# Blank matmuls between the first transposes, a step moved ahead of a transpose, and one slot more for the arrival of loads, in a kernel of two sliding-window attention blocks

## The chip, the cores and the metric

The kernel runs on one core of a Trainium2 chip. The metric is the device time in microseconds (us) of one execution. The engines are TensorE (PE; its weight loads are shown as PEld), VectorE (DVE), ScalarE (ACT), GpSimd (POOL) and SyncE (SP), which here issues nearly all of the transfers.

## The reference

Two independent problems A and B of the same form are computed, and their outputs are put side by side. Each is a multi-head attention block with a causal sliding window:

```
B, S, D = 1, 2048, 1024;  H = 32 heads;  Dh = 32;  W = 256
q, k, v = split(x @ wqkv)                      # each S x D, in heads of 32
scores = (q @ k.T) * Dh**-0.5                  # per head
mask   = (0 <= i - j) & (i - j < W)            # query i, key j
p      = softmax(where(mask, scores, -1e9))
out    = concat_heads(p @ v) @ wo              # S x D
result = concat([out_A, out_B], axis=-1)
```

All inputs and outputs are bf16.

## The kernel before, in words

Sequence positions are cut into 16 blocks of 128, and these into four groups of four (512 positions, index k). Heads are taken four at a time (a head group g, 128 columns of q, k or v; eight for each problem, 16 in all). x is held transposed, as `xT[(problem, k)]` with 8 slices of 128 input columns (`ct`), because TensorE contracts over partitions.

Projections are cut into chains (`_Chain`): a chain for Q or K of one head group and 512 positions is eight matmuls, one for each `ct`, accumulated in one PSUM bank (`qk_steps`, tile `pp`, two buffers), then copied out by ACT or DVE (`evacuate`, line 188). V chains (`v_steps`) serve two head groups (index m) and two blocks, in 16 matmuls of 256 columns. Chains of the output projection (`out_steps`, `last_steps`) end in a store. `by_columns` (line 170) issues a step either as one matmul (line 172) or as four of 32 columns that run side by side (line 176).

Attention runs in 180 slots, the loop over `now` from line 600. In each slot, `session` (line 438) computes scores of four block pairs for four heads (line 451, PSUM tile `st`, one buffer), ACT takes their exponentials (line 459, tile `pt`), and POOL clears what the mask forbids (lines 467 and 471). Three slots later `pv` (line 486) multiplies with V and with ones, the second for the sums of the softmax (line 513, tile `acc`). DVE adds edge blocks (line 481), takes the reciprocal of the sums (line 524), spreads it (line 529) and multiplies (line 531).

What is left of a slot on TensorE is filled with steps of chains, by a planner that runs when the program is built. Each chain has an `early` and a `late` slot. `start_chain` takes the ready chain (`early <= now`) with the smallest `late`. `level` (line 426) sets how many nanoseconds of work a slot gets, from the listed durations `NS_MM`, `NS_ROW` and `NS_PV`. Its result is the smallest, over later slots d, of the work that becomes ready before d divided by the slots up to d; work with a later `early` is so kept out of the sum for smaller d.

Loads after the first are cut into pieces and put into slots by the loop at line 331. POOL writes a zero to the piece's place (line 350), which orders it, and SP issues the load: for B's x as transposing transfers (line 133), in two pieces for each block. The dictionary `arrival` holds the slot from which chains may use a load: the slot of its last piece plus 2. `landed` (line 342) hands it to the chains' `early` (lines 360, 365 and 375). The x of problem A and the first weights have arrival slots set by hand (lines 328 and 329).

The head of the program is written out by hand. ACT's queue issues the first Q weights. SP's queue issues, in this order, x blocks 0 and 1 as plain rows, the first K weights, x blocks 2 and 3, V weights, then transposing loads of A's later x groups with weights between them (lines 541 to 562). While these come in, TensorE runs five matmuls on a blank tile of zeros (`top`, seen as `blank`, lines 564 to 566). Then `flip(a)` transposes block a on TensorE (eight transposes of 128 by 128 into one PSUM bank, line 578), and ACT (line 582) and after it DVE (line 583) copy a half each into `xT[(0, 0)]`. `first(which, lo)` (line 585) does the eight steps of the first Q (0) or K (1) chain for 256 of its 512 columns: columns 0 to 255 need flips 0 and 1, columns 256 to 511 need flips 2 and 3. The last of these is followed by the first V chain.

Of the kernel before, what the change touches and what calls it, by code (L numbers as in the profile page):

```python
# [18 lines left out]
P = 128  # L19
# [59 lines left out]
def _fast_path(ctx, tc, cfg, problems, outs, consts, certify):  # L79
    nc = tc.nc  # L80
# [40 lines left out]
    xT, wqk, wv, wo_sb, vts, oTs, qks, pts = {}, {}, {}, {}, {}, {}, {}, {}  # L121
# [4 lines left out]
    blank = top[:].bitcast(BF16)  # L126
# [71 lines left out]
    def qk_steps(g, which, k, lo=0, hi=512, st_=None, last=True):  # L198
        pi = g // T
        st_ = {} if st_ is None else st_  # L200
        steps = []
        for ct in range(CT):
            def f(ct=ct):
                if "pp" not in st_:
                    st_["pp"] = new_pp()
                by_columns(st_["pp"], lo, hi, wqk[g][:, ct, which, :], xT[(pi, k)][:, ct, lo:hi],
                           ct == 0, ct == CT - 1)
                clock.pe += NS_MM * (hi - lo) / 512.0
                if ct == CT - 1 and last:
                    dst = qk_tiles(g)[which][:, k * 512:(k + 1) * 512]  # L210
                    evacuate(dst, st_["pp"][:])
                    add_or(dst)
            steps.append((NS_MM * (hi - lo) / 512.0, f))
        return steps
# [108 lines left out]
    def entries_of(now):  # L323
        return [(n // NE,) + entries[n % NE]
                for n in range(now * SLOTS, min((now + 1) * SLOTS, G * NE))]

    pieces = {}
    arrival = {("x", 0, k): t for k, t in ((2, 3), (3, 5))}
    arrival.update({("wqk", 1): 1, ("wv", 1): 4})
    free = 0  # L330
    for time, key, fs in wanted:
        free = max(free, time)
        new = fs[0]
        for where, f in fs[1:]:
            while len(pieces.get(free, [])) >= min(2 if key[0] == "x" else SLOTS, sum(
                    q != j + 1 for _, j, q in entries_of(free))):
                free += 1
            pieces.setdefault(free, []).append((new, where, f))
            new = None
        arrival[key] = free + 2  # L340

    def landed(*key):
        return arrival.get(key, 0)
# [218 lines left out]
            load_wv(1, 0, CT, nc.sync)  # L562

    warm = ps_proj.tile([P, 512], F32, name="pp")
    for _ in range(5):
        nc.tensor.matmul(warm[:], lhsT=blank[:, 0:P], rhs=blank[:, 0:512], start=True, stop=True)
    flips = [ps_acc.tile([P, 512], F32, name="acc") for _ in range(2)]
    flips = [f[:] for f in flips]
    flips.append(ps_st.tile([P, 4, SLOTS, P], F32, name="st")[:, 0].rearrange("p a q -> p (a q)"))
# [3 lines left out]
    def flip(a):  # L573
        if a == 3:
            flips[a] = ps_acc.tile([P, 512], F32, name="acc")[:]
        f = flips[a].bitcast(BF16).rearrange("p (ct q) -> p ct q", q=P)
        for ct in range(CT):
            nc.tensor.transpose(out=f[:, ct, :], in_=xrow[a][:, ct * P:(ct + 1) * P],  # L578
                                identity=ident[:])
        dst = xT[(0, 0)][:, :, a * P:(a + 1) * P]  # L580
        half = CT // 2
        nc.scalar.copy(out=dst[:, :half, :], in_=f[:, :half, :])
        nc.vector.tensor_copy(out=dst[:, half:, :], in_=f[:, half:, :])

    def first(which, lo):
        for _, f in qk_steps(0, which, 0, lo, lo + 256, held[which], last=lo > 0):
            f()

    flip(0)
    flip(1)  # L590
    flip(2)
    first(0, 0)
    flip(3)
    first(1, 0)
    first(0, 256)
# [4 lines left out]
    for now in range(END):  # L600
# [3 lines left out]
        while due and due[0][0] <= now:  # L604
            _, pg, pk = due.pop(0)
# [14 lines left out]
    while due:  # L620
        _, pg, pk = due.pop(0)
# [132 lines left out]
def kernel(  # L754
# [48 lines left out]
    with tc.manual_schedule():  # L803
        with ExitStack() as fctx:
            _fast_path(fctx, tc, cfg, problems, outs, consts, [reduce_bits, decide])
# [40 lines left out]
```

## Time and profile before

| what | value |
|---|---|
| median of 9 runs | 612.51 us (611.1 to 614.17) |
| profiled execution, its own time | 612.31 us |
| its span, first to last instruction | 610.6 us |
| TensorE busy | 599.7 us, 98% |
| VectorE, ScalarE, GpSimd busy | 463.6, 445.2, 328.1 us |
| instructions | 28789 |

The span is the stretch that the profile's views are told in: a time in them counts from its start. In a view in order of time, a line gives the start, the duration of the group, the engine, the line of the program, the operation, what is written and what is read, shapes, and how many instructions were merged (x8). Behind it in brackets stands the idle time of the engine ahead of it and what ended that. A duration of a group ends with the drain of its last matmul; the distance from one start to the next is the time for which TensorE is taken. A line of the waits gives the total in microseconds, how often, and the longest. "SPq" is the queue of SP that issues transfers. Granted clock is the share of TensorE's full clock that the profile shows.

### The profile page before, as it was taken

What the parts mean: (1) busy time and instruction counts of PE and PEld (TensorE: products, weight loads), DVE (VectorE), ACT (ScalarE), POOL (GpSimd) and SP (SyncE); (2) the same over time, 40 slices, a digit from 0 to 9 for tenths busy, and PEclk for the clock granted to TensorE, in tenths of its full rate; (3) what the DMA queues carried; (4) which work ended last, traced back from release to release, by engine and by line L of the source; (5) the groups of instructions that cost most, each with busy time, mean ns of one, the idle gap of its engine ahead of it and who ended that gap; (6) DMA issues with size and microseconds to landing.
All of it is one profiled execution on the core that took longest, in us unless ns stands there. A gap on an engine that the chain in (4) does not pass through costs nothing.

```text
span 610.6 us, 28789 instructions
## 1 busy us (share of the span) xinstructions
PE 599.7 (98%) x12824; PEld 345.4 (57%) x12824; DVE 463.6 (76%) x1193; ACT 445.2 (73%) x382; POOL 328.1 (54%) x630
## 2 busy tenths in 40 slices
PE   7999999999999999999999999999999999999996
PEld 5555466656654765654565756755445664545443
DVE  1577888887899889878888889698987978897200
ACT  3777878888887777877777777777776878776332
POOL 0565666666656666565555656555565556555000
PEclk9999999999999999999999999999999999999999
DMA  9923110111015510444111000112011030113221
GB/s 242 172 76 103 37 38 4 38 38 39 3 33 85 111 25 6 87 97 99 37 38 38 21 21 2 39 37 81 2 57 44 3 106 20 55 52 125 71 78 64
DMA packets 86802, 35.47 MB, mean 58 GB/s; under 512 B 65552, under 2 KB 86160, under 8 KB 86672
## 3 DMA queue, kind: packets, MB, share of 16 engines
q1 hardware_dynamic: 85632, 33.31, 22.6%
q8 instruction: 102, 1.67, 1.1%
q10 hardware_dynamic: 1040, 0.26, 0.2%
q14 instruction: 28, 0.23, 0.1%
HBM read 17.83 MB, written 8.39 MB: 43 GB/s over the span
## 4 chain that ended last, share of the span: by engine, by line
PE 95%; ACT 2%; DMA 1%; issue 0%; SPq 0%; POOL 0%; ACTq 0%
PE pp L176 43%; PE pp L172 29%; PE acc L513 13%; PE st L451 10%; ACT pt L459 2%; DMA oT<-in_A_x_dram 1%; DMA xT<-in_B_x_dram 0%; ACT vt L190 0%; PE st L578 0%; ACT kT L190 0%; PE acc L578 0%; SPq L548 0%; POOL pt L471 0%; ACT qT L190 0%; SPq L145 0%
## 5 line engine op out<-in xcount | busy, mean ns | idle before, releaser
L459 ACT ACTIVATE pt<-st 128x2048 bf16<-128x2048 f32 x180 | 338.0, 1878 | 86.5 <-PE st L451 70.4
L471 POOL TENSOR_SCALAR_AFFINE_SELECT pt<-pt 128x512 bf16<-128x512 bf16 x224 | 155.9, 696 | 145.7 <-ACT pt L459 145.7
L467 POOL TENSOR_SCALAR_AFFINE_SELECT pt<-pt 128x512 bf16<-128x512 bf16 x256 | 179.3, 702 | 87.0 <-ACT pt L459 87.0
L524 DVE RECIPROCAL rinv<-acc 128x128 f32<-128x128 f32 x128 | 121.8, 952 | 57.1 <-PE acc L513 56.6
L176 PE MATMUL pp<-xT,wqk 128*32 128x512 bf16 x2728 | 164.1, 379 | 1.0 <-DVE both L481 0.7
L481 DVE TENSOR_TENSOR both<-pt 128x512 bf16<-128x512 bf16 x224 | 138.1, 656 | 0.0
L176 PEld LDWEIGHTS <-wqk 128*32 128x32 bf16 x2728 | 69.8, 97 | 55.9 <-DVE both L481 0.9
L172 PE MATMUL pp<-xT,wqk 128*128 128x512 bf16 (+1 forms) x358 | 82.6, 374 | 0.8 <-ACT kT L190 0.4
L176 PE MATMUL pp<-wv,xT 128*32 128x256 bf16 x2436 | 75.6, 273 | 0.0
L451 PE MATMUL st<-qT,kT 32*128 32x384 bf16 (+2 forms) x1488 | 71.5, 269 | 0.0
L176 PEld LDWEIGHTS <-xT 128*32 128x32 bf16 x2436 | 63.8, 97 | 5.2
L529 DVE STREAM_SHUFFLE wide<-rinv 128x128 f32<-128x128 f32 x256 | 64.5, 297 | 0.0
L513 PE MATMUL acc<-pt,vt 128*32 128x128 bf16 (+1 forms) x2160 | 63.4, 239 | 0.0
L172 PE MATMUL pp<-wo_sb,oT 128*128 128x512 bf16 (+1 forms) x288 | 62.4, 374 | 0.0
L451 PEld LDWEIGHTS <-kT 32*128 32x128 bf16 x1488 | 22.2, 92 | 65.3 <-issue 63.8
L190 ACT CAST osb<-pp 128x512 bf16<-128x512 f32 (+1 forms) x54 | 31.1, 576 | 38.4 <-PE pp L172 26.9
L531 DVE TENSOR_TENSOR oT<-acc,wide 128x256 bf16<-128x256 f32 x128 | 54.3, 424 | 4.4
L176 PE MATMUL pp<-wo_sb,oT 128*32 128x512 bf16 x928 | 54.6, 379 | 0.0
L172 PEld LDWEIGHTS <-wqk 128*128 128x128 bf16 x358 | 33.4, 99 | 36.8 <-issue 6.9
L172 PE MATMUL pp<-wv,xT 128*128 128x256 bf16 x415 | 51.0, 273 | 0.4 <-ACT kT L190 0.2
L513 PEld LDWEIGHTS <-vt 128*32 128x32 bf16 x2160 | 35.9, 96 | 26.3 <-issue 24.0
L172 PEld LDWEIGHTS <-xT 128*128 128x128 bf16 x415 | 38.9, 98 | 11.6 <-issue 5.1
(46 smaller groups left out, 382.2 us busy)
## 6 DMA issues: line engine op xcount, KB each, us to landing
out_dram<-osb SPq DMA_DIRECT2D x63, 128.0 KB, 1.8
wqk<-in_B_wqkv_dram SPq DMA_DIRECT2D x32, 128.0 KB, 2.6
wqk<-in_A_wqkv_dram SPq DMA_DIRECT2D x24, 128.0 KB, 2.7
wo_sb<-in_A_wo_dram SPq DMA_DIRECT2D x16, 128.0 KB, 2.2
wv<-in_B_wqkv_dram SPq DMA_DIRECT2D x16, 128.0 KB, 2.6
wo_sb<-in_B_wo_dram SPq DMA_DIRECT2D x16, 128.0 KB, 2.5
oT<-in_A_x_dram SPq DMA_DIRECT2D x4, 256.0 KB, 4.8
wv<-in_A_wqkv_dram SPq DMA_DIRECT2D x2, 512.0 KB, 5.0
```

The costliest lines, as they stand in the source:

```text
L172: nc.tensor.matmul(out[:, lo:hi], lhsT=lhsT, rhs=rhs, start=start, stop=stop, skip_group_check=True)
L176: nc.tensor.matmul(out[c:c + 32, lo:hi], lhsT=lhsT[:, c:c + 32], rhs=rhs, start=start, stop=stop, tile_position=(0, c), skip_group_check=True)
L190: nc.scalar.copy(out=out, in_=in_)
L451: nc.tensor.matmul(st[:, r, a:b, :], lhsT=kT[32 * r:32 * r + 32, j * P:(j + 1) * P], rhs=qT[32 * r:32 * r + 32, q * P:(q + b - a) * P], st ...
L459: nc.scalar.activation(out=pt[:, :, :n, :].rearrange("p r a q -> p r (a q)"), in_=st[:, :, :n, :].rearrange("p r a q -> p r (a q)"), func= ...
L467: nc.gpsimd.affine_select(out=blk, in_=blk, pattern=[[0, 4], [1, P]], compare_op=ALU.is_ge, fill=0.0, base=0, channel_multiplier=-1)
L471: nc.gpsimd.affine_select(out=blk, in_=blk, pattern=[[0, 4], [-1, P]], compare_op=ALU.is_gt, fill=0.0, base=0, channel_multiplier=1)
L481: nc.vector.tensor_tensor(out=both[:, :, h, :], in0=pts[s0][:, :, a0, :], in1=pts[s1][:, :, a1, :], op=ALU.add)
L513: nc.tensor.matmul(acc[32 * r:32 * r + 32, o:o + w_], lhsT=lhsT, rhs=src[:, r, :, :], start=(x == 0), stop=(x == len(moves) - 1), tile_pos ...
L524: nc.vector.reciprocal(out=rinv[:], in_=acc[:, 2 * P:3 * P])
L529: nc.vector.stream_shuffle(out=wide[:, h * P:(h + 1) * P], in_=rinv[:], mask=[16 * h] * 32)
L531: nc.vector.tensor_tensor(out=oTs[(pi, k)][:, t, (p % 2) * 256:(p % 2 + 1) * 256], in0=acc[:, 0:256], in1=wide[:], op=ALU.mult)
```

## The change

Three edits. After the loop that places the loads, arrival of the x of problem B and of later V weights is the last piece's slot plus 3 in place of 2; that of the other weights stays at plus 2. In the head, six blank matmuls in place of five run ahead of the first flip, four more follow flip 0, and three more follow flip 1. And the first Q step, `first(0, 0)`, comes ahead of `flip(2)` rather than behind it.

```diff
@@ -337,7 +337,7 @@
                 free += 1
             pieces.setdefault(free, []).append((new, where, f))
             new = None
-        arrival[key] = free + 2
+        arrival[key] = free + (3 if key[0] in ("x", "wv") else 2)
 
     def landed(*key):
         return arrival.get(key, 0)
@@ -562,8 +562,12 @@
             load_wv(1, 0, CT, nc.sync)
 
     warm = ps_proj.tile([P, 512], F32, name="pp")
-    for _ in range(5):
-        nc.tensor.matmul(warm[:], lhsT=blank[:, 0:P], rhs=blank[:, 0:512], start=True, stop=True)
+
+    def keep_warm(n):
+        for _ in range(n):
+            nc.tensor.matmul(warm[:], lhsT=blank[:, 0:P], rhs=blank[:, 0:512], start=True, stop=True)
+
+    keep_warm(6)
     flips = [ps_acc.tile([P, 512], F32, name="acc") for _ in range(2)]
@@ -587,9 +591,11 @@
             f()
 
     flip(0)
+    keep_warm(4)
     flip(1)
+    keep_warm(3)
+    first(0, 0)
     flip(2)
-    first(0, 0)
     flip(3)
     first(1, 0)
     first(0, 256)
```

## The prediction

> **What bounds the kernel now.** I read the page's busy times and its chain first, then the engine's waits, then the order of time at the two places where TensorE waits. The page:
>
> ```profile
> PE 599.7 (98%) x12824; PEld 345.4 (57%) x12824; DVE 463.6 (76%) x1193; ACT 445.2 (73%) x382; POOL 328.1 (54%) x630
> ...
> PE 95%; ACT 2%; DMA 1%; issue 0%; SPq 0%; POOL 0%; ACTq 0%
> ```
>
> TensorE is busy for 599.7 of 610.6 us and is 95% of the chain that ends last. Its work is not changed by order, so the time can only move by the 10.9 us in which it does nothing, and by stretches in which it works slowly. Its waits, longest first:
>
> ```profile
> PE pp L566 <- DVE ones L777: 1.3, 1, 1.3
> PE acc L578 <- DMA oT<-in_A_x_dram: 1.0, 2, 0.9
> PE st L578 <- DMA oT<-in_A_x_dram: 0.8, 1, 0.8
> PE pp L176 <- DVE both L481: 0.7, 1, 0.7
> ...
> PE pp L176 <- DMA xT<-in_B_x_dram: 0.3, 1, 0.3
> ```
>
> The first three lie in the head, the last two around 260 us. The head, TensorE alone, in order of time (start, duration, count behind x):
>
> ```profile
> 3.81 1.04 PE L578 MATMUL acc<-ident,oT 128*128 128x128 bf16 x8 [0.18 <-DMA oT<-in_A_x_dram]
> 5.70 1.03 PE L578 MATMUL acc<-ident,oT 128*128 128x128 bf16 x8 [0.86 <-DMA oT<-in_A_x_dram]
> 7.50 1.04 PE L578 MATMUL st<-ident,oT 128*128 128x128 bf16 x8 [0.77 <-DMA oT<-in_A_x_dram]
> 8.33 1.91 PE L172 MATMUL pp<-xT,wqk 128*128 128x256 bf16 x8
> 10.04 1.06 PE L578 MATMUL acc<-ident,oT 128*128 128x128 bf16 x8
> 10.89 2.87 PE L172 MATMUL pp<-xT,wqk 128*128 128x256 bf16 x24
> ```
>
> Blocks 1 and 2 of x arrive at 5.70 and 7.50. The eight 256-column matmuls from 8.33 take 1.71 us to the next start, 0.213 each; the later ones go 0.107 apart (the chain has 40 in 4.41). So TensorE runs at half speed up to 10.89, although the granted-clock column reads 1.00 there; its rate doubles 3.39 us after it began to work without a gap at 7.50. The first stretch, 1.31 to 4.85 with one gap of 0.18, didn't raise it. At the other end the same delay is in the clock column: the last matmul ends at 605.04 and the clock halves inside 608 to 609 (mean 0.70, so at 608.4).
>
> The second place, all engines in order of time:
>
> ```profile
> 258.65 2.52 SPq L133 DMA_TRANSPOSE xT<-in_B_x_dram  x2
> ...
> 260.36 0.28 PE L513 MATMUL acc<-both,ones 128*32 128x128 bf16 x8
> ...
> 261.39 1.05 PE L176 MATMUL pp<-xT,wqk 128*32 128x512 bf16 x16 [0.74 <-DVE both L481]
> ...
> 262.73 1.48 PE L176 MATMUL pp<-xT,wqk 128*32 128x512 bf16 x24 [0.29 <-DMA xT<-in_B_x_dram]
> ```
>
> The last two pieces of x(1,2) are issued at 258.65 and 259.96 and take 2.7 and 2.5 us to land, so at 261.35 and 262.48, just before the two restarts. The profile names DVE for the first; the landing fits better, as these matmuls read nothing of that addition.
>
> **The change, part by part.** All is set against the profiled execution's own 612.31 us (610.6 span and 1.7 around it), which stands 0.2 under the median 612.51.
>
> *Blank matmuls and the moved step.* One more blank matmul of 512 columns costs 0.427 us at half speed (1.31, 1.72, 2.14 are starts): six end their issue at 3.87, where block 0 had let the transposes start at 3.81, so 0.06. Four more cost 1.71 at half speed or 0.86 at full (0.216 each, as eleven 512-column ones in 2.48 later on), three more 1.28 or 0.65. Only TensorE issues any of this: no DMA moves. SP goes on with its transposing loads (3.77 on), POOL waits for the first exponential (17.98); ACT and DVE keep their order of copies. The new wait: the first Q matmuls now follow the second flip directly and need its copies, ACT 0.585 and then DVE 0.42, with 0.04 before each, so 0.62 and 1.08 after it drains (0.19 after its last issue). Queued behind on TensorE are the third and fourth flips, and ACT and DVE wait for these; three blanks cover 0.65 to 1.28 of it.
>
> The unknown is when the clock rises. TensorE now works from 1.31 almost without a gap. By the 3.39 us the earliest is 4.7. The stretch that failed says that it need not be so early; a span of 3.39 that begins at an unlucky moment is surely filled by 8.1. No row rules out 10.89 as before. I take the middle of the first two, 6.4. A transpose goes 0.107 apart at half speed; at full speed no row shows it: between 0.107 (unchanged) and 0.054; I take 0.06, as the 256- and 512-column matmuls both halve. Then: flip 0 to 4.73; four blanks to 6.44; flip 1 to 6.93, drained 7.1; ACT's copy to 7.72, DVE's to 8.18; Q matmuls, four from 7.76 and four to 8.65; flips 2 and 3 (blocks landed 7.5 and 8.2) to 9.14 and 9.63; K matmuls to 10.49; flip 3's copies end 10.55 and 11.01; Q's second half from 10.59 to 11.48; K's to 12.34. There V starts, at 13.61 in the profile (wv's last packets are read at 9.2, so it is there): 1.27 us gained. With the clock up at 4.7 the same walk ends at 11.59 (2.02 gained), at 8.1 at 12.93 (0.68 gained), at 10.89 at 14.23 (0.62 lost); unhalved transposes add up to 0.9 where they lie on the path.
>
> What is late next: x(0,3), issued on SP at 20.16 and landed at 29.56 whatever TensorE does. Its first reader is the third of nine four-way steps in the stretch from 30.57, at 31.00, so 1.44 us are free. 1.27 fits; of 2.02, 0.58 is given back. So the head is worth 1.27, from 1.44 gained to 0.62 lost.
>
> [...]
>
> *The later arrival.* Loads stay in their slots; only the planner's "early" of chains moves, and only where it binds. Working the plan of before through from its own constants: every V chain is ready at least a slot early, and of x only x(1,2) (arrival 84, both its first chains start in slot 84) and x(1,3) (90) are used at once. Slot 84 begins at 259.58: this is the stall. Without it the first step would have come at 260.48 (0.12 behind the sums' first, as at 264.92 and 265.04) and came at 261.39, 0.91 lost; four steps at 0.216 end at 262.25, the fifth came at 262.73, 0.48 lost. Together 1.39 us of issue. A slot later (2.81 us) the first reader stands at about 263.3, 0.8 behind the landing, so all of it goes: 1.39, bounds 0 and 1.39.
>
> The price: the work ready before slot 84 sets the budget of slots 0 to 83 (2831 ns, where later slots get about 3050). It is now spread over 85: (2831 x 84 + 940) / 85 = 2809, 22 ns less in each, 1.9 us moved behind slot 84. TensorE bounds both sides (49.5 to 49.9 of 50 us busy between 50 and 250), so the move costs nothing; if a slot couldn't shrink, ACT (41.2 of 50) or DVE (43.1) would have to be full, and it would cost the 1.9. Steps fall in other slots from the start; the waits for evacuations between 150 and 250 us (0.3, 0.2, 0.4) may double or vanish: plus or minus 0.9, taken as 0.
>
> Sum: 612.31 - 1.27 - 1.39 = 609.65.
>
> **Rivals.**
> *The blanks don't raise the clock* (zeros, or transposes between them that count for nothing). For it: the first stretch of blanks didn't. Against it: the filled 3.39 us with its transposes did. Then blanks run at half speed, flip 1 ends its issue at 7.29, Q starts at 8.57, flip 3 ends at 11.98, and the clock rises between 12 and 18.8: V starts at 14.56 (clock at 12), at 16.26 (15.4), and at 18.8 the loss is 4.35 with V's first matmuls slow too. Less 1.39, the times are 611.9, 613.6 and 615.3; I take 614.4, slower. It decides from a clock later than about 12.9.
> *The stall stays* (the loads slip with the slot, or another chain waits for the same x): only the head's gain, 611.0. For it: SP spends 12.35 us on eight transposing loads, more than four slots. Against it: 0.8 us of margin.
> *The shorter slots don't shrink*, ACT or DVE binding: 609.65 + 1.9 = 611.55. Against it: the busy times above.
> *The order of all slots comes out worse*: to undo the gain, some nine more waits of 0.3 us; 612.3, more would be slower. In 300 to 568 us TensorE waits for nothing.
>
> **How the numbers follow.** A 0.2% step (1.2 us) is about what a measurement of this kernel tells from no change: faster is under 611.3, slower over 613.7. Forecast 0.61, with 608.6 (1.44 and 1.39 and 0.9 better) to 611.8 (head nothing, waits 0.9 worse) as its own range; clock rival 0.13; stall stays 0.12; slots don't shrink 0.07; worse order 0.07. Faster: 0.58 + 0.08 + 0.02 + 0.01 = 0.69. Slower: 0.07 of the clock rival and 0.02 of the worse order, 0.09. Same: 0.22. Range: 608.6 to 612.2 takes in the forecast, the second and third rivals but 0.01, and a little of the others, 0.81.
>
> **What would show it.** Right: 256-column matmuls 0.107 apart from the first Q step on; V's first at about 12.3; no wait of line 176 for B's x near 260 and its first reader in slot 85; no wait for A's x near 29. Wrong: spacing of 0.213 past 9 us, a wait for the copies longer than the blanks cover, or new waits for ACT and DVE before 250 us.

## The result, and the profile after

The changed kernel takes 609.49 us (median of 13 runs, 609.07 to 610.23), against 612.43 us for the kernel before (40 runs, 611.1 to 614.51). The ratio is 0.995, with a 95% interval of 0.9942 to 0.9959; by the ratio that is 3.1 us faster, between 2.5 and 3.6. The forecast was 609.65 us. The profiled execution took 609.58 us, with a span of 607.9, so 2.73 us less than the one before.

The page of the changed kernel, busy times and chain:

```profile
PE 598.5 (98%) x12838; PEld 344.0 (57%) x12838; DVE 468.4 (77%) x1199; ACT 441.1 (73%) x376; POOL 326.6 (54%) x630
...
PE 96%; ACT 2%; DMA 1%; issue 0%; SPq 0%; ACTq 0%
```

TensorE still bounds the kernel. It stands idle for 9.4 us of the span (607.9 less 598.5) in place of 10.9, and it works at half speed for a shorter time (up to 4.16 in the trace's clock record, in place of 11.07). The edits push lines down: the blanks are now line 568, the flips 582 with their copies from 586. TensorE's waits (total, how often, longest):

```profile
PE pp L568 <- DVE ones L783: 1.3, 1, 1.3
PE pp L172 <- ACT vt L190: 1.0, 2, 0.5
PE pp L172 <- ACT kT L190: 0.6, 2, 0.4
PE acc L582 <- DMA oT<-in_A_x_dram: 0.5, 2, 0.4
```

The two lines of line 176 around 260 us are gone, and of the waits for blocks of x 0.5 us are left out of 1.8. The waits for ACT to empty a bank have grown to 1.6 us, where the profile before has 1.1:

```profile
PE pp L172 <- ACT kT L190: 0.6, 2, 0.4
PE pp L172 <- ACT vt L190: 0.3, 1, 0.3
PE pp L172 <- ACT qT L190: 0.2, 1, 0.2
```

The head of the changed kernel, TensorE in order of time:

```profile
1.32 2.74 PE L568 MATMUL pp<-top 128*128 128x512 bf16 x6 [1.32 <-DVE ones L783]
4.22 0.62 PE L582 MATMUL acc<-ident,oT 128*128 128x128 bf16 x8 [0.16 <-DMA oT<-in_A_x_dram]
4.67 1.03 PE L568 MATMUL pp<-top 128*128 128x512 bf16 x4
6.08 0.62 PE L582 MATMUL acc<-ident,oT 128*128 128x128 bf16 x8 [0.38 <-DMA oT<-in_A_x_dram]
6.54 0.81 PE L568 MATMUL pp<-top 128*128 128x512 bf16 x3
7.38 1.05 PE L172 MATMUL pp<-xT,wqk 128*128 128x256 bf16 x8
8.27 0.61 PE L582 MATMUL st<-ident,oT 128*128 128x128 bf16 x8
8.71 0.61 PE L582 MATMUL acc<-ident,oT 128*128 128x128 bf16 x8
9.16 2.81 PE L172 MATMUL pp<-xT,wqk 128*128 128x256 bf16 x24
11.80 1.91 PE L172 MATMUL pp<-wv,xT 128*128 128x256 bf16 x16
```

Starts give the pace: flip 0 goes from 4.22 to 4.67, 0.056 for a transpose, and the Q step from 7.38 to 8.27, 0.111 for a matmul with its one short stop. So TensorE runs at full speed from the first flip on. V starts at 11.80, where it started at 13.61.

The second place, all engines in order of time, some lines of it:

```profile
256.24 0.40 PE L451 MATMUL st<-qT,kT 32*128 32x384 bf16 x8
...
257.03 0.28 PE L513 MATMUL acc<-both,ones 128*32 128x128 bf16 x8
257.14 1.92 PE L176 MATMUL pp<-wv,xT 128*32 128x256 bf16 x64
...
258.99 0.40 PE L451 MATMUL st<-qT,kT 32*128 32x256 bf16 x8
...
259.77 0.28 PE L513 MATMUL acc<-both,ones 128*32 128x128 bf16 x8
259.88 2.33 PE L176 MATMUL pp<-xT,wqk 128*32 128x512 bf16 x40
```

Slot 84 begins at 256.24. In the profile before it began with this line:

```profile
259.58 0.40 PE L451 MATMUL st<-qT,kT 32*128 32x384 bf16 x8
```

In the changed kernel slot 84 holds V steps (257.14), and the first readers of x(1,2) come in slot 85, at 259.88, right behind the sums and with no wait.

Between the two profiles the head gives 13.61 - 11.80 = 1.81 us, the stall 1.39, and 0.5 is given back in waits for ACT: 2.70 of the measured 2.73.

### The profile page after: what moved, and what is told of

Read it like the earlier page. It is cut to its first block, busy times and chain, and to the rows that moved or that the text cites. A ratio compares the mean times of both kernels' runs of the same rounds, so it can differ in the third digit from the quotient of the medians.

```text
span 607.9 us, 28820 instructions
## 1 busy us (share of the span) xinstructions
PE 598.5 (98%) x12838; PEld 344.0 (57%) x12838; DVE 468.4 (77%) x1199; ACT 441.1 (73%) x376; POOL 326.6 (54%) x630
## 4 chain that ended last, share of the span: by engine, by line
PE 96%; ACT 2%; DMA 1%; issue 0%; SPq 0%; ACTq 0%
PE pp L176 44%; PE pp L172 29%; PE acc L513 13%; PE st L451 10%; ACT pt L459 1%; DMA oT<-in_A_x_dram 1%; PE acc L582 0%; ACT vt L190 0%; ACT kT L190 0%; PE pp L568 0%; PE st L582 0%; SPq L548 0%; ACT osb L190 0%; PE pp L805 0%; ACTq L190 0%
```

## The experiments

The theory is that of the prediction, with two gains that don't depend on each other: the clock of TensorE rises early in the head, and the stall on x(1,2) goes. The rivals are named with each run. All ratios are to the kernel before, run beside on the same chip; its median was 612.91 us for e1 to e4, 612.34 for e5 to e8 and 613.27 for e9 to e12. A ratio need not be the quotient of the two medians to the last digit.

**The two halves.** First the arrival edit alone (e1_arrival), and the head's edits alone (e2_head).

```diff
# e1_arrival
-        arrival[key] = free + 2
+        arrival[key] = free + (3 if key[0] in ("x", "wv") else 2)
```

> Only the arrival of x and wv is moved a slot later; the head is that of before. Theory (two independent gains): the two waits before the first readers of x(1,2) near 260 us go, 1.39 us, less 0.5 for more waits on evacuations that the changed kernel shows before 250 us (1.4 us idle there against 0.9): 0.9 us faster than before, ratio about 0.9985, V's first matmul at 13.6 as before. Rival (the gain is all the head's, and the stall only moves): ratio 1.000 and new waits of about 1.4 us elsewhere.

```diff
# e2_head
-    for _ in range(5):
-        nc.tensor.matmul(warm[:], lhsT=blank[:, 0:P], rhs=blank[:, 0:512], start=True, stop=True)
+    keep_warm(6)
...
     flip(0)
+    keep_warm(4)
     flip(1)
+    keep_warm(3)
+    first(0, 0)
     flip(2)
-    first(0, 0)
```

> Only the head's edits (six, four and three blanks, first Q step ahead of flip 2); arrival as before. Theory: V's first matmul at about 11.8 in place of 13.6, the plan of before with its waits near 260 us unchanged: 1.8 us faster less up to 0.4 if x(0,3) is waited for, ratio 0.9970 to 0.9977; with the gain of the arrival alone it sums to the changed kernel's 2.9. Rival (the two parts overlap, since an earlier head makes loads late): 2.5 to 2.9 or under 1.2.

e1_arrival: 611.87 us, ratio 0.9982 (0.9971 to 0.9993), 1.1 us faster. Its waits hold no line for B's x, and the same 1.6 us for ACT as the changed kernel:

```profile
PE pp L172 <- ACT vt L190: 1.0, 2, 0.5
...
PE pp L172 <- ACT kT L190: 0.6, 2, 0.4
```

So these come with the new order of the slots, and not with the head. e2_head: 610.88 us, ratio 0.9963 (0.9951 to 0.9975), 2.3 us faster, with V at 12.08. That is above the 1.4 to 1.8 that the theory gave; the interval takes in 1.8 and reaches into the first rival's range. The two halves add up to 0.0055, the changed kernel has 0.0050 (0.0041 to 0.0058). An overlap of the parts isn't seen, though the intervals would hide one of a few tenths of a microsecond, and neither half alone is the gain.

**Which load.** Only x(1,2) gets the later slot, in the kernel before (e6_x12) and in the changed kernel (e12_x12).

```diff
# e6_x12, against the kernel before
-        arrival[key] = free + 2
+        arrival[key] = free + (3 if key == ("x", 1, 2) else 2)
# e12_x12, against the changed kernel
-        arrival[key] = free + (3 if key[0] in ("x", "wv") else 2)
+        arrival[key] = free + (3 if key == ("x", 1, 2) else 2)
```

> Only the arrival of x(1,2) a slot later, nothing else of the change. Theory (this load alone made the wait near 260 us): as the whole arrival edit, ratio about 0.998, no wait for B's x. Rival (V weights or the other x groups matter too): ratio 0.999 or more.

> The changed kernel with only the arrival of x(1,2) a slot later, V weights and other x groups as before. Theory (only that load binds): equal to the changed kernel within 0.0005, the same waits for ACT of 1.6 us in all, none for B's x. Rival (V weights' later arrival matters): 0.001 or more above it.

e6_x12: 611.85 us, ratio 0.9990 (0.9980 to 1.0000). The ratio itself lies at the rival's edge (0.999 or more), and the interval takes in both, so the time doesn't decide. e12_x12: 609.80 us, 0.9943 (0.9929 to 0.9956), beside 0.9948 (0.9934 to 0.9962) for the changed kernel in the same series (e11_again). Neither has a wait for B's x, and both have the 1.6 us for ACT. In the programs as built the two arrival edits order TensorE's instructions alike but for one short stretch. So x(1,2) is the load that bound, and the later arrival of V weights and the other x groups does nothing that can be measured.

**The head's parts.** The move alone (e3_move), the blanks alone (e4_blanks), and the sixth blank alone (e5_six), each in the kernel before.

```diff
# e3_move
     flip(0)
     flip(1)
-    flip(2)
     first(0, 0)
+    flip(2)
# e4_blanks
-    for _ in range(5):
-        nc.tensor.matmul(warm[:], lhsT=blank[:, 0:P], rhs=blank[:, 0:512], start=True, stop=True)
+    keep_warm(6)
...
     flip(0)
+    keep_warm(4)
     flip(1)
+    keep_warm(3)
     flip(2)
     first(0, 0)
# e5_six
-    for _ in range(5):
-        nc.tensor.matmul(warm[:], lhsT=blank[:, 0:P], rhs=blank[:, 0:512], start=True, stop=True)
+    keep_warm(6)
...
     flip(0)
     flip(1)
```

> Only the move: five blanks, none between, first Q step ahead of flip 2. Theory (the clock is what the head gains): without blanks TensorE stands idle until flip 1's copies are done at about 7.8, Q then takes 1.71 at half speed, flips 2 and 3 come after it, and the clock rises only 3.4 us after 7.8, so at 11.2: V starts at 13.6 to 14.5, ratio 1.000 to 1.0015. Rival (the head gains by using the wait for block 2): V starts 0.8 us earlier than before, ratio 0.9987.

> Only the blanks (six, four, three), the Q step behind flip 2 as before. Theory (the clock): it rises near 4.2 as in the changed kernel; flip 2 waits for block 2 to 7.5, Q follows from 8.0 to 8.9, flip 3 to 9.3, K to 10.2, Q's and K's second halves wait for flip 3's copies at 10.5 and end near 12.2: 1.3 to 1.6 us faster than before, ratio 0.9975 to 0.998. Rival (the move matters as much): 0.9 us or less, ratio 0.9985 or more.

> Only the sixth blank matmul; nothing else. [...] Times in two groups, median between: ratio 0.998 to 0.9995. Rival (it takes 3.4 us without any gap): the clock never rises before 10.9, ratio 1.000.

e4_blanks: 611.22 us, ratio 0.9971 (0.9961 to 0.9980), 1.8 us faster, V at 12.17: the blanks alone bring most of the head's gain. That is a little more than the theory's 1.3 to 1.6 us, which the interval takes in, and the rival's 0.9 or less lies outside it.

e3_move: 612.34 us, ratio 0.9986 (0.9972 to 1.0000). Its profile shows the wait that the blanks stand in front of in the changed kernel:

```profile
7.76 1.87 PE L172 MATMUL pp<-xT,wqk 128*128 128x256 bf16 x8 [0.67 <-ACT xT L582]
9.42 1.06 PE L578 MATMUL st<-ident,oT 128*128 128x128 bf16 x8
10.27 1.06 PE L578 MATMUL acc<-ident,oT 128*128 128x128 bf16 x8
11.12 3.51 PE L172 MATMUL pp<-xT,wqk 128*128 128x256 bf16 x24
14.47 1.80 PE L172 MATMUL pp<-wv,xT 128*128 128x256 bf16 x15
```

The Q step takes 1.66 us to the next start, half speed as the theory says. The 24 matmuls from 11.12 take 3.35 us, where e2_head has 2.64 for them at full speed, which puts the rise at an estimated 12.6, later than the theory's 11.2, and V starts at 14.47. e1_arrival, which has the head of before, starts V at 14.32, and its 24 matmuls in 3.06 us put the rise at an estimated 12.1. In the profile the move gains nothing, while the ratio lies where the rival put it, with an interval that ends at 1. This run doesn't decide.

Its profile also shows the old stall on x(1,2) under another name:

```profile
262.45 1.05 PE L176 MATMUL pp<-xT,wqk 128*32 128x512 bf16 x16 [0.94 <-POOL wv L350]
263.66 1.48 PE L176 MATMUL pp<-xT,wqk 128*32 128x512 bf16 x24 [0.16 <-POOL wv L350]
```

Five profiles keep the old arrival (before, e2_head, e3_move, e4_blanks, e5_six). Ahead of the first restart they name DVE three times and POOL twice, but in all five both restarts come 0.2 to 0.3 us behind the landing of a piece of x(1,2): in the profile before at 261.39 and 262.73, behind landings at 261.15 and 262.46. The two waits add up to between 0.6 and 1.1 us, so the profile before, with 1.0, is one of the longer ones.

e5_six: 612.39 us, ratio 0.9997 (0.9986 to 1.0009), less than the expected 0.998 to 0.9995; the ratio is the rival's, although the clock did rise early, which the rival rules out. The times, 610.77 to 613.45, don't show the two groups, which were the author's estimate. The profile tells why the gain is missing. Here the granted-clock column (the figure before the last two, behind the busy times of the five engines) shows a fall, where the pace of starts shows none in any other profile's head:

```profile
7.00:8.00 1.00, 0.06 (x1) 0.06 (x2) 0.42 (x1) 0.39 (x1) 0.00 (x0) 1.00 1.06 357
...
8.80:9.00 0.20, 0.20 (x3) 0.18 (x2) 0.00 (x0) 0.20 (x1) 0.00 (x0) 0.56 1.20 284
9.00:10.00 1.00, 1.00 (x8) 0.76 (x6) 0.42 (x1) 0.18 (x1) 0.00 (x0) 0.50 1.40 244
10.00:12.00 2.00, 2.00 (x15) 1.61 (x13) 0.42 (x1) 0.58 (x1) 0.00 (x0) 0.50 1.23 277
12.00:13.00 1.00, 1.00 (x10) 0.83 (x8) 0.00 (x0) 0.00 (x0) 0.00 (x0) 0.88 1.28 291
```

And TensorE in the same stretch:

```profile
4.24 1.03 PE L582 MATMUL acc<-ident,oT 128*128 128x128 bf16 x8 [0.19 <-DMA oT<-in_A_x_dram]
6.14 0.62 PE L582 MATMUL acc<-ident,oT 128*128 128x128 bf16 x8 [0.87 <-DMA oT<-in_A_x_dram]
7.94 0.62 PE L582 MATMUL st<-ident,oT 128*128 128x128 bf16 x8 [1.18 <-DMA oT<-in_A_x_dram]
8.40 1.50 PE L172 MATMUL pp<-xT,wqk 128*128 128x256 bf16 x8
```

The clock was up by 6.14 (flip 0 takes 1.03, flips 1 and 2 take 0.62 each), but TensorE waited 0.87 and 1.18 for blocks 1 and 2, the clock went down at 8.82 (0.56 in the mean of 8.80 to 9.00), and it came back at 12.24 (0.88 in the mean of 12 to 13), 3.4 us later. In this profile the clock rises behind six blanks and flip 0, but it doesn't stay up behind the waits for the blocks; with the blanks between the flips it stayed up in every profile (0.61 to 0.62 for a flip, 0.11 for a matmul of the first Q step).

**How many blanks are needed.** The changed kernel without the four and three (e7_six_move), with five first ones (e8_five), without the three alone (e10_no_three), and with all blanks but the old place of the Q step (e9_no_move), beside the changed kernel once more (e11_again).

```diff
# e7_six_move, against the changed kernel
     flip(0)
-    keep_warm(4)
     flip(1)
-    keep_warm(3)
     first(0, 0)
# e8_five
-    keep_warm(6)
+    keep_warm(5)
# e10_no_three
-    keep_warm(3)
     first(0, 0)
# e9_no_move
     keep_warm(3)
-    first(0, 0)
     flip(2)
+    first(0, 0)
```

> The changed kernel without its four and three blanks between the flips. [...] Rival (the sixth blank does all of it): 0.995.

> The changed kernel with five first blanks in place of six. [...] Rival (it takes 3.4 us without any gap, so from 4.2 on): rise between 7.6 and 11, 1 us lost: 0.9968 or more.

> The changed kernel once more, as the reference for the three beside it: ratio 0.995, V's first matmul between 11.8 and 12.6.

> The changed kernel without the three blanks ahead of the first Q step; its work is otherwise the same. [...]

> The changed kernel with the first Q step behind flip 2, as before. Theory (the move is worth what flip 2 waits for block 2): block 2 lands at 7.5 to 7.9, some 0.4 us after Q could have started, and V starts 0.4 us later than in the changed kernel: ratio 0.0005 to 0.0008 above it. Rival (the move is worth nothing): equal to it.

| run | median us | ratio (95%) |
|---|---|---|
| e7_six_move | 611.07 | 0.9975 (0.9964 to 0.9986) |
| e8_five | 609.45 | 0.9954 (0.9936 to 0.9972) |
| e11_again | 609.90 | 0.9948 (0.9934 to 0.9962) |
| e10_no_three | 609.88 | 0.9944 (0.9931 to 0.9958) |
| e9_no_move | 610.10 | 0.9952 (0.9938 to 0.9965) |

Without the blanks between the flips about half of the gain is lost (e7_six_move, with times from 609.35 to 612.39). The rival's 0.995 lies outside the interval: the sixth blank doesn't do it all. With them, it doesn't matter in what can be measured whether five or six go first, whether the three are there, and where the Q step stands; the 0.0004 between e9_no_move and e11_again is a little under what was expected of the move, and lies well inside the intervals. e8_five's clock rose at an estimated 6.9 (flip 1 takes 0.51 us to the next start, where all at full speed takes 0.45), before the rival's 7.6. V in e11_again started at 12.65, just later than the 11.8 to 12.6 expected. In e10_no_three the place of the three is an idle wait for the copies:

```profile
6.83 0.64 PE L582 MATMUL acc<-ident,oT 128*128 128x128 bf16 x8
8.14 1.06 PE L172 MATMUL pp<-xT,wqk 128*128 128x256 bf16 x8 [0.67 <-ACT xT L586]
9.03 0.61 PE L582 MATMUL st<-ident,oT 128*128 128x128 bf16 x8
```

The clock stays up across these 0.67 us of idle time (starts 0.111 and 0.056 apart behind it). No version beats the changed kernel by what can be told; the parts that carry it are the blanks between the flips and the slot of x(1,2). The four are enough without the three (e10_no_three); no run has the three without the four.

## Why the prediction was right, point by point

- *TensorE bounds, so only its idle and its slow stretches count.* Right: the chain is 96% TensorE, and 2.70 of 2.73 us are found in those places between the two profiles.
- *The clock rises at 6.4, not before 4.7, at the latest by 8.1.* That filled gaps bring the rise forward was right, and the upper bound, the author's estimate of twice 3.39 us from 1.31, held; the lower bound and the rule behind it were wrong. The prediction read a delay of 3.39 us from the start of work without a gap, and saw the same delay at the end (605.04 to 608.4). The trace's record has the rise of the profile before at 11.07, not 10.89, and in the profile after the clock falls 2.91 us behind the last matmul's end (601.99 to 604.90), against 3.36 in the profile before: no fixed delay is shown. The record has the rise at 4.16 in the changed kernel's profile, 2.84 us behind TensorE's first matmul at 1.32, so 3.39 us of filled work weren't needed there. By the pace of starts the rise comes at an estimated 4.5 in e4_blanks, 5.3 to 5.7 in e2_head, and 6.5 to 7.3 in the five profiles e8_five to e12_x12 (last section). That 6.4, a middle taken between two bounds, lies near these is in part luck.
- *V starts at 12.34.* It was 11.80 in the profile after, and with the same head 12.08 (e2_head), 12.65 (e11_again) and 12.94 (e12_x12): a mean of 12.37. Given the rise, the walk of the head holds: between its 12.34 (clock at 6.4) and 12.93 (at 8.1) it gives an estimated 12.60 for e11_again, where the pace of starts puts the rise at 7.15, and which had 12.65. With the early rise of the profile after it is too fast (11.59 for 4.7): flip 0 came at 4.22 and block 1 at 6.08, later than the 3.87 and 5.70 it took from the profile before. The head's term of 1.27 was 1.81 between the two profiles, and by the runs 2.3 (1.5 to 3.0): it was too small. The profile before had V at 13.61; two others of the same old head had it at 14.32 (e1_arrival) and 14.45 (e6_x12). The profile that the prediction started from had its clock up soon, at 11.07 against an estimated 12.1 and 12.5 by the pace of starts.
- *A transpose at full speed takes 0.06.* It took 0.056.
- *x(0,3) is late next, with 1.44 us free.* No wait came. It landed at 28.9 (issued 19.70, 9.2 to landing), and its first reader, the third step from 28.77, comes at 29.20: 0.3 us to spare. SP reached this load half a microsecond sooner than before, as the transposing load ahead of it took 6.01 us of its time in place of 6.86.
- *The stall of 1.39 goes as a whole.* No wait is left, and the first reader stands in slot 85, 2.0 us behind the last landing (255.42 plus 2.5) where 0.8 was forecast. That the landing was behind the wait which the profile gave to DVE is borne out by the five profiles above, and by e6_x12, where a later slot for the readers of this one load takes both waits away. The prediction put the first landing at 261.35; the piece issued at 258.65 took 2.5 us, not 2.7, and was there at 261.15. By the time, the arrival edit alone is worth 1.1 us (0.4 to 1.8), its new waits for ACT included.
- *22 ns less in each of slots 0 to 83, at no cost.* Slot 84 begins 259.58 - 256.24 = 3.34 us earlier, 1.81 of it from the head; with the 0.5 of new waits added back, 2.0 over 84 slots are 24 ns each. TensorE is busy for all of 250 to 568 us (50.00 of 50.00 us between 250 and 300, where it was 48.96). The slots did shrink, and the rival that had ACT or DVE bind falls.
- *Waits for evacuations, plus or minus 0.9, taken as 0.* They cost 0.5.
- *The rivals.* That blanks don't raise the clock falls with e4_blanks (up at an estimated 4.5, in place of 11.07 in the profile before); that the stall stays falls with e1_arrival. The worse order of slots shows in the 0.5 us of new waits, where the rival needed some nine more of 0.3.

So the total fell on the forecast with a head underrated by some 0.5 us (by the two profiles) and waits for ACT of 0.5 us that were left out, and these two cancel. That the sum is so close is luck of that kind; its two main terms are each shown by a run of their own.

Open: what the move alone is worth. Three pairs differ by it alone, all to its favour: e3_move and the kernel before by 0.0014, e2_head and e4_blanks by 0.0008, e11_again and e9_no_move by 0.0004. Each difference lies within the intervals; e3_move's alone reaches from nothing to 1.7 us.

## What to carry to other kernels

Where the first transfers come in one by one, TensorE's idle time cost twice here: once as a wait, and once more as half speed afterwards (e5_six: waits of 0.87 and 1.18 us, then 3.4 us at half speed). Work without use in these gaps was worth its issue time where it stood in the long gaps (e4_blanks, 1.8 us faster), and not where it stood only ahead of the first (e5_six, ratio 0.9997). And a wait that a profile gives to one engine should be held against the landing of the loads that the waiting instruction reads, since a planner's estimate that is a slot short for a single load cost about 1 us of 612 here.

## What the runs showed of the hardware that was not expected

The clock of TensorE didn't rise at one delay from the start of work. The rises of the two profiles before and after are those of the trace's record, the second one of e5_six is from its granted-clock column; the others are estimated from starts, as a group of matmuls that takes longer than the same group at full speed:

| profile | clock up at, us | V from, us |
|---|---|---|
| after | 4.16 | 11.80 |
| e4_blanks | 4.5 | 12.17 |
| e2_head | 5.3 to 5.7 | 12.08 |
| e5_six | 5.3 to 6.1, and again at 12.24 | 14.00 |
| e9_no_move | 6.5 | 12.37 |
| e8_five | 6.9 | 12.55 |
| e10_no_three | 6.8 to 6.9 | 12.57 |
| e11_again | 7.15 | 12.65 |
| e12_x12 | 7.3 | 12.94 |
| e7_six_move | 9.5 | 12.80 |
| before | 11.07 | 13.61 |
| e1_arrival | 12.1 | 14.32 |
| e6_x12 | 12.5 | 14.45 |
| e3_move | 12.6 | 14.47 |

The profiles after and e11_again are of the same kernel, with six blanks from 1.32 and 1.31 and flip 0 at 4.22 and 4.19, and their rises lie 3.0 us apart. So the work on TensorE alone doesn't tell the moment, and what sets it was not shown. Nor is the delay of a fall one figure: 3.36 us behind the last matmul's end in the profile before, 2.91 in that after. In e5_six the fall at 8.82 comes 0.88 us after TensorE went back to work at 7.94. The 3.4 us at half speed that follow cost an estimated 1.7 us, half of them. The old kernel's runs spread by 3.4 us (611.1 to 614.51), the changed kernel's by 1.2; how much of either is the moment of the rise, and how much the landing of the first blocks, no run separates.

The granted-clock column reads 1.00 up to the first change on record, whatever the clock was: the profile before has 1.00 in 8.50 to 9.50, where 256-column matmuls start 0.213 apart. The pace of starts is the sure reading.
